# A transformer layer on one core: weights of Q, K and V ahead of later tokens, three gate products on GpSimd, small filling matmuls

## The chip, the cores and the metric

The kernel runs on one core of a Trainium2 chip. The metric is the time of one execution in device microseconds; the runs of the kernel before have a median of 182.08 us.

## The reference

One layer: adaptive layer norm, dilated local attention, a second adaptive norm, a feed-forward block; S = 2048 tokens, D = 448, 16 heads of 28, F = 1792, all in bf16.

```python
mod = (_silu(c) @ w_mod).reshape(c.shape[0], 6, 1, -1)
sa, ca, ga, sb, cb, gb = (mod[:, 0].copy(), ..., mod[:, 5].copy())
h = _layernorm(x, axis=-1) * (1 + ca) + sa
x = x + ga * _A_ref(h, A_wqkv, A_wo)
h = _layernorm(x, axis=-1) * (1 + cb) + sb
x = x + gb * _B_ref(h, B_w1, B_w2)
```

`_A_ref` projects to q, k, v, lets each token attend to itself and the seven even-distance tokens before it (distance 2, 4, ... 14), and projects by `wo`; `_B_ref` is `silu(x @ w1) @ w2`.

## The kernel before, in words

The tokens are cut into four chunks of 512 (k = 0 to 3 in the code; first to fourth below), each held as even and odd tokens, so that the dilated window becomes a dense band in each parity. Attention works on nine blocks of 112 to 128 tokens of a parity. Per chunk there are these stages:

- `Norm` (L443): the statistics of each 128-token tile are taken on VectorE (L455, L456; "b") or on ScalarE (sum L459 and square L465, with the mean on GpSimd at L462 between them; "a"). GpSimd makes the reciprocal root and the scaled shift (L469 to L476), and VectorE or ScalarE writes the normalised tokens `xn` (L485, L483). In the second pair of tiles of the third and fourth chunk the statistics are ScalarE's.
- transposes: the first chunk on TensorE (L513) with scale and shift at L520 and L522; later ones by DMA issued from SP (L535), with scale and shift at L540 and L542. The result is `h`. Scale and shift (`modc`) come from L419, which needs the silu of c; that is turned on TensorE at L404.
- projection: V at L643, Q and K at L619 into pairs of PSUM tiles `ps_qk`; the evacuations are L632 (V) and L623 (Q and K). The Q/K weights are first padded to 32 per head by VectorE (L550, L552).
- attention: logits L671, exponential on ScalarE L679, band mask on VectorE L703, values L729, normalisation L734 and L735, DMA transposes L739, output projection L763 and residual L766.
- feed-forward: L790, silu and evacuation on ScalarE L794, L812, residual L817, store L820.

The gates ga and gb are not applied to the tokens: `wo` and `w2` are multiplied by them once. For `w2` this is L844, seven products of 128 x 896, all on VectorE before.

All PSUM tiles of two banks (`ps_w`, `ps_t`, `ps_v`, `ps_qk`, `ps_l`, `ps_h`, `ps_wo`) come from one pool of three buffers, in turn. A tile that comes third in line waits until the tile before it in that buffer was read.

The order of all work is written out by hand: `ORDER` (L42) lists the operations by number, and `emit` (L195) records them in that order; a "v" or "a" behind a number picks VectorE or ScalarE. Each engine then works through its own queue in that order, and an instruction that waits holds up everything behind it on its engine. Loads are issued by SP at L334. While TensorE has nothing to do at the start, it multiplies a tile of zeros, `junk` (`warm_up`, L387): `WARM` products in one go and ten operations of two each, placed by `ORDER`.

Of the kernel before, what the change touches and what calls it, by code (L numbers as in the profile page):

```python
# [32 lines left out]
CP = 256  # L33
BLOCKS = ((0, 1), (2, 3), (4, 5), (6, 7, 8))
HW = 128 + CP
WARM, JUNK = 7, 10
HOW1 = ("bbbb", "bbbb", "bbaa", "bbaa")
HOW2 = ("ssss", "ssss", "ssss", "ssss")
SEQ = "e0 e1 e2 e3 e4 s0 e5 e6 s1 e7 e8 s2 s3"


ORDER = (  # L42
# [32 lines left out]
def half(j):  # L75
    return slice(K3 * j, K3 * j + K3)
# [140 lines left out]
def layer(ctx, tc, io, safe):  # L217
# [3 lines left out]
    A_x, A_wqkv, A_wo, B_w1, B_w2, c, w_mod, out = io  # L221
    nc = tc.nc
    V, S, G, T = nc.vector, nc.scalar, nc.gpsimd, nc.tensor
# [10 lines left out]
    def ct(shape, name, dt=BF16):  # L234
        return const.tile(shape, dt, name=name)

    def bigt(name):
        return big.tile([128, 2, 512], F32, name=name, tag="big")
# [21 lines left out]
    junk = both[:, KT * 6 * D:KT * 6 * D + 512]  # L260
    w1 = ct([128, 3, F], "w1")
    w13 = ct([128, F // 2], "w13")
    w2 = ct([128, NF, D], "w2")
# [43 lines left out]
    P = Plan()  # L307
# [20 lines left out]
    def sp(ns, fn, deps, land=0.0, give=()):  # L328

        a = P.op(("sp", ns), fn, deps, take=("dma",))  # L330
        return P.op(("none", land), none, [a], give=((a, "dma"),) + tuple(give)), a
# [52 lines left out]

    warm = []

    def warm_up(n):  # L387
        if not warm:
            warm.append(bigt("ps_w"))
        for _ in range(n):  # L390
            T.matmul(warm[0][:, 0, :], lhsT=junk[:, 0:128], rhs=junk, start=True, stop=True)
    w_first = P.op(("pe", 600.0), none, take=("big",))
    w_last = P.op(("pe", 213.0 * WARM), lambda o: warm_up(WARM), [w_first], mac=213.0 * WARM)
    junks = [P.op(("pe", 428.0), lambda o: warm_up(2), [w_last], mac=426.0) for _ in range(JUNK)]

    P.op(("none", 0.0), none, junks, give=((w_first, "big"),))

# [11 lines left out]
    def mod_cols(vecs, dst0, loads):  # L409

        ps = {}

        def mm(o):
            ps[0] = one.tile([128, 2, KT], F32, name="ps_m", tag="one")
            for i, v in enumerate(vecs):
                for j in range(KT):
                    c0 = v * D + ROW[j]
                    for k in range(KT):
                        T.matmul(ps[0][:, i, j:j + 1], lhsT=wmod[:, k, c0:c0 + 128], rhs=scT[:, k:k + 1], start=(k == 0), stop=(k == KT - 1))  # L419

        def ev(o):
            V.tensor_copy(out=modc[:, dst0, :], in_=ps[0][:, 0, :])
            V.tensor_scalar(out=modc[:, dst0 + 1, :], in0=ps[0][:, 1, :], scalar1=1.0, scalar2=None, op0=ALU.add)
        a = P.op(("pe", 900.0), mm, [sct] + loads, take=("one",))
        return P.op(("dve", 150.0), ev, [a], give=((a, "one"),))
# [3 lines left out]
    def gate(i, v, loads):  # L429
        ps = {}  # L430

        def mm(o):
            ps[0] = onet("ps_g")
            for k in range(KT):
                T.matmul(ps[0][:, 0:D], lhsT=screp[:, k, :], rhs=wmod[:, k, v * D:(v + 1) * D], start=(k == 0), stop=(k == KT - 1))
        a = P.op(("pe", 760.0), mm, [rep] + loads, take=("one",), mac=653.0)
        wmod_read.append(a)
        return P.op(either(430.0, 540.0), lambda o: copy_on(o)(out=gbc[:, i, :], in_=ps[0][:, 0:D]), [a], give=((a, "one"),))  # L438
# [154 lines left out]
    def norm1(k):  # L593
        h = h1[k % NH]
        after = [x for kk in (k - NH,) if kk >= 0 for x in qk_mm[kk] + v_mm[kk] + [halo[kk + 1]]] + (pads if k == 2 else [])

        n = Norm([4 * k + j for j in range(4)], {4 * k + j: ld_x[k][j // 2] for j in range(4)}, after=after, n=2, how=HOW1[k], scratch=both[:, KT * 6 * D + 512:KT * 6 * D + 512 + D])

        def out_of(k):
            return h[:, :, k, 128:128 + CP]  # L600
        if k:
            n.on_dma(lambda j: h[:, :, :, 128 + 64 * j:256 + 64 * j].rearrange("p t k s -> p (t k) s"), out_of, 0, [mod1])
        else:
            n.on_pe((0, 2, 1, 3), out_of, lambda ps: ps.rearrange("p (t s) -> p t s", t=2), [mod1], True)
        h1_done[k] = list(n.done)
        if k:
            w = 32 * k
            halo[k] = P.op(either(60.0 + 0.83 * 8 * w, 60.0 + 0.26 * 8 * w), lambda o: copy_on(o)(out=h[:, :, :, 128 - w:128].rearrange("p t k s -> p (t k) s"),
                                                                                               in_=h1[(k - 1) % NH][:, :, :, 128 + CP - w:128 + CP].rearrange("p t k s -> p (t k) s")), h1_done[k - 1] + after)
# [223 lines left out]
    for k in range(NC):  # L833
        norm1(k)
        project(k)
        if k == 0:
            g_o = gate(0, 2, ld_mo)
            g_2 = gate(1, 5, ld_m2)
            mod2 = mod_cols((3, 4), 2, ld_mb)
            wmod_read.append(mod2)  # L840
            wo_gated = [P.op(("dve", 1030.0), lambda o: V.tensor_tensor(out=wo[:, 0], in0=wo[:, 0], in1=gbc[:, 0, :].unsqueeze(1).to_broadcast([128, KT, D]), op=ALU.mult), [g_o] + ld_o)]
            wo_gated += [sp(550.0, f, wo_gated[0:1], 1500.0)[0] for f in (lambda o: nc.sync.dma_start(out=wo[half(1), 1, :, :], in_=wo[half(0), 0, :, :]),
                                                                      lambda o: nc.sync.dma_start(out=wo[half(0), 1, 1:4, :], in_=wo[half(1), 0, 0:3, :]))]
            w2_gated = [P.op(("dve", 535.0), lambda o, f=f: V.tensor_tensor(out=w2[:, f:f + 2, :], in0=w2[:, f:f + 2, :],  # L844
                                                                             in1=gbc[:, 1, :].unsqueeze(1).to_broadcast([128, 2, D]), op=ALU.mult), [g_2, ld_2[f // 8]])
                        for f in range(0, NF, 2)]

# [47 lines left out]
@with_exitstack  # L895
def kernel(
    ctx: ExitStack,
    tc: tile.TileContext,
    A_x: bass.AP,
    A_wqkv: bass.AP,  # L900
    A_wo: bass.AP,
    B_x: bass.AP,
    B_w1: bass.AP,
    B_w2: bass.AP,
    c: bass.AP,
    w_mod: bass.AP,
    out: bass.AP,
):
    io = (A_x, A_wqkv, A_wo, B_w1, B_w2, c, w_mod, out)
    with ExitStack() as first:  # L910
        with tc.manual_schedule():
            bad = layer(first, tc, io, False)
    with tc.If(bad > 0, label="safe"):
        with ExitStack() as again:
            layer(again, tc, io, True)
# [30 lines left out]
```

## Time and profile before

| what | value |
|---|---|
| median of two runs | 182.08 us (181.75 to 182.41) |
| span of the profiled execution, first to last instruction | 179.6 us |
| what lies around the span, by the median | 2.48 us |
| TensorE busy | 168.7 us, 94% of the span |
| VectorE, ScalarE, GpSimd busy | 103.9, 110.1, 26.1 us |
| mean granted TensorE clock | 0.994 |

The profiled execution has no time of its own besides its span. In the profile's rows the engines are PE (TensorE), PEld (its weight loads), DVE (VectorE), ACT (ScalarE), POOL (GpSimd) and SP (SyncE, which issues most DMAs; SPq is its queue). A timeline row has start, length, engine, line, operation, output and inputs, and a count; in square brackets stands how long the engine was idle before it and whose work ended that. TensorE's products are pipelined, so the last of a row shows a tail of some 0.2 to 0.4 us that overlaps the next row. In rows of the chain of waits only start, length, engine, tile and line are given.

### The profile page before, as it was taken

The numbers are of one execution on the slowest core, as the hardware profiler recorded it, in microseconds if no ns is written. First come the engines' busy times: TensorE is split into PE (matmuls) and PEld (weight loads), VectorE is DVE, ScalarE is ACT, GpSimd is POOL, SyncE is SP. The second block draws the span as 40 slices with busy tenths as digits, with TensorE's granted clock in tenths as the row PEclk, the third lists the DMA queues.
The fourth block names the chain that finished last, engine by engine and source line by source line (L and its number), as shares of the span: only waits on it lengthen the run. The fifth ranks groups of instructions, "written<-read, shape, count | busy, mean of one in ns | idle before, by whom it ended". The sixth has DMA issues, their size and how long they took to land.

```text
span 179.6 us, 3554 instructions
## 1 busy us (share of the span) xinstructions
PE 168.7 (94%) x1406; PEld 76.7 (43%) x1406; DVE 103.9 (58%) x219; ACT 110.1 (61%) x153; POOL 26.1 (15%) x86
## 2 busy tenths in 40 slices
PE   7999999888889999999999999999999998999990
PEld 2543333444345344344544445554434444434540
DVE  5699797699798988364378135984633311200211
ACT  2277939897779657779999649643596322244200
POOL 4656540000012220022000000023040000000000
PEclk9999999999999999999999999999999999999997
DMA  5993569956682223102400013125307000010021
GB/s 199 333 344 89 143 143 305 336 117 152 185 251 55 51 62 84 26 0 62 58 26 4 26 26 80 29 55 135 84 0 194 5 0 26 0 51 4 29 79 35
DMA packets 33343, 17.42 MB, mean 97 GB/s; under 512 B 24296, under 2 KB 32936, under 8 KB 33320
## 3 DMA queue, kind: packets, MB, share of 16 engines
q1 hardware_dynamic: 33168, 16.90, 35.0%
q8 instruction: 13, 0.21, 0.5%
q10 hardware_dynamic: 152, 0.23, 0.4%
q14 instruction: 10, 0.08, 0.2%
HBM read 9.12 MB, written 1.84 MB: 61 GB/s over the span
## 4 chain that ended last, share of the span: by engine, by line
PE 70%; DVE 10%; DMA 7%; ACT 6%; POOL 3%; issue 2%; SPq 0%; ACTq 0%; DVEq 0%
PE ps_h L790 25%; PE ps_y L812 24%; PE ps_wo L763 7%; PE ps_qk L619 5%; PE ps_v L643 4%; ACT p L679 2%; PE ps_o L729 2%; DMA oT<-o 2%; DMA x_all<-in_A_x_dram 2%; DVE p L703 2%; DVE st L455 2%; PE ps_l L671 2%; ACT xn L483 2%; DMA wqk<-xn 2%; DMA h<-xn 2%
## 5 line engine op out<-in xcount | busy, mean ns | idle before, releaser
L790 PE MATMUL ps_h<-h,w 128*128 128x512 bf16 (+1 forms) x224 | 47.3, 380 | 0.0
L812 PE MATMUL ps_y<-w,both 128*128 128x448 bf16 x224 | 46.1, 353 | 0.6 <-DVE flag L884 0.6
L794 ACT ACTIVATE both<-ps_h 128x1024 bf16<-128x1024 f32 x28 | 28.0, 1022 | 26.0 <-PE ps_h L790 25.9
L679 ACT ACTIVATE p<-ps_l 128x896 bf16<-128x896 f32 (+1 forms) x36 | 30.7, 933 | 2.2 <-PE ps_l L671 2.1
L812 PEld LDWEIGHTS <-both 128*128 128x128 bf16 x224 | 20.8, 98 | 20.6 <-issue 1.6
L790 PEld LDWEIGHTS <-w 128*128 128x128 bf16 (+1 forms) x224 | 16.9, 96 | 27.0 <-issue 11.4
L817 DVE TENSOR_TENSOR ot<-ps_y,x_all 128x448 bf16<-128x448 f32 x16 | 9.8, 621 | 30.2 <-PE ps_y L812 30.1
L619 PE MATMUL ps_qk<-h,wp 128*128 128x512 bf16 (+1 forms) x96 | 20.0, 380 | 0.4 <-DVE h L542 0.4
L703 DVE TENSOR_TENSOR p<-p,maskb 128x1792 bf16<-128x1792 bf16 (+1 forms) x18 | 19.5, 1098 | 0.5 <-ACT p L679 0.5
L465 ACT ACTIVATE screp<-x_all,mv 128x448 bf16<-128x448 bf16 x16 | 10.7, 666 | 9.9 <-POOL mv L462 9.5
L619 PEld LDWEIGHTS <-wp 128*128 128x128 bf16 (+1 forms) x128 | 9.3, 97 | 16.1 <-issue 6.1
L462 POOL TENSOR_SCALAR mv<-sums 128x2 f32<-128x2 f32 x10 | 3.4, 343 | 76.0 <-DVE x_all L766 75.9
L766 DVE SCALAR_TENSOR_TENSOR x_all<-ps_wo,x_all 128x448 bf16<-128x448 f32 x16 | 9.5, 620 | 7.7 <-PE ps_wo L763 7.7
L485 DVE TENSOR_SCALAR xn<-x_all,mv,rs 128x512 bf16<-128x512 bf16 x23 | 8.8, 406 | 8.6 <-POOL rs L472 8.4
L763 PE MATMUL ps_wo<-wo,oT 128*128 128x448 bf16 (+1 forms) x64 | 12.5, 354 | 1.0 <-DMA oT<-o 0.6
L643 PE MATMUL ps_v<-wv,h 128*128 128x448 bf16 (+1 forms) x56 | 11.1, 354 | 1.0 <-ACT p L679 0.7
L623 DVE CAST qk<-ps_qk 128x1024 bf16<-128x1024 f32 x10 | 12.0, 1214 | 0.1
L472 POOL TENSOR_TENSOR rs<-rs,negh 128x2 f32<-128x2 f32 x16 | 11.5, 717 | 1.3
L735 DVE TENSOR_TENSOR o<-ps_o,rc 112x448 bf16<-112x448 f32 (+1 forms) x18 | 11.2, 624 | 0.6
L729 PE MATMUL ps_o<-v,p 128*128 128x29 bf16 x288 | 9.6, 176 | 1.2 <-DVE gbc L438 0.6
L542 DVE TENSOR_SCALAR h<-h,modc 128x512 bf16<-128x512 bf16 x15 | 5.6, 407 | 8.6 <-DMA h<-xn 8.6
L729 PEld LDWEIGHTS <-p 128*128 128x128 bf16 x288 | 8.8, 96 | 4.1 <-DVE p L703 0.9
(85 smaller groups left out, 147.9 us busy)
## 6 DMA issues: line engine op xcount, KB each, us to landing
out_dram<-ot SPq DMA_DIRECT2D x16, 112.0 KB, 1.7
both<-in_w_mod_dram SPq DMA_DIRECT2D x2, 672.0 KB, 5.7
x_all<-in_A_x_dram SPq DMA_DIRECT2D x3, 448.0 KB, 5.8
w<-in_B_w_dram SPq DMA_DIRECT2D x3, 448.0 KB, 6.0
w<-in_B_w_dram SPq DMA_DIRECT2D x1, 896.0 KB, 5.0
both<-in_w_mod_dram SPq DMA_DIRECT2D x2, 336.0 KB, 3.4
w<-in_B_w_dram SPq DMA_DIRECT2D x1, 672.0 KB, 5.2
wv<-in_A_wqkv_dram SPq DMA_DIRECT2D x2, 224.0 KB, 5.0
```

What stands on the lines that cost most here:

```text
L472: G.tensor_tensor(out=rs[:, j:j + n], in0=rs[:, j:j + n], in1=negh[:, 0:n], op=ALU.pow)
L619: T.matmul(ps[:, j, :], lhsT=w.rearrange("p h d -> p (h d)"), rhs=h[rows, :, t, 128:128 + CP], start=start, stop=stop)
L623: return [(either(act_ns(1024), dve_ns(1024)), lambda o, ps: copy_on(o)(out=qk[:, :, g, :, s0:s0 + CP], in_=ps[:].rearrange("p j (t s) -> ...
L643: T.matmul(ps[:, par, 0:D], lhsT=h[rows, par, t, b0:b0 + 128], rhs=wv[rows, t, :], start=(kk == ks[0]), stop=(kk == ks[-1]))
L679: S.activation(out=out_, in_=ps[:, :, 0:4 * nq].rearrange("p j (g q) -> p j g q", q=nq), func=ACTF.Exp, scale=SCALE)
L703: V.tensor_tensor(out=p, in0=p, in1=maskb[:, 1 if b == 0 else 0, 0:nq].unsqueeze(1).to_broadcast([128, H, nq]), op=ALU.mult)
L729: T.matmul(ps[:, h, 0:DH + 1], lhsT=p[:, at:at + 128], rhs=v[:, h, 0:DH + 1], start=True, stop=True)
L735: V.tensor_tensor(out=box["o"][0:nq, off:off + D].rearrange("p (h d) -> p h d", d=DH), in0=ps[0:nq, :, 0:DH], in1=r.unsqueeze(2).to_broadc ...
L763: T.matmul(ps[:, par, 0:D], lhsT=oT[rows, kk, par, s0:s0 + 128], rhs=wo[rows, par, kk, :], start=(q == qs[0]), stop=(q == qs[-1]))
L790: T.matmul(ps[:, j, :], lhsT=w, rhs=h[rows, :, t, :], start=start, stop=stop)
L794: return [(("act", act_ns(1024)), lambda o, ps: S.activation(out=hid[:, k % 2, :, i, :], in_=ps[:], func=ACTF.Silu), after + f2_read.get(k ...
L812: T.matmul(box["ps"][:, 0:D], lhsT=hid[:, k % 2, f % 2, f // 2, 128 * j:128 * j + 128], rhs=w2[:, f // 2 + 7 * (f % 2), :], start=(f == 0) ...
```

## The change

Three things change.

First, `ORDER`: the loads of the Q, K and V weights (operations 13 to 20 as numbered there) go out right behind the first chunk's tokens and the modulation weights, ahead of the second and third chunk's tokens. The steps that hang on them move too: on VectorE the scale and shift of the first chunk and the padding of the weights now come before the statistics of the second chunk, and on ScalarE the statistics of the third chunk come after the normalisation of the second.

On SP at the start, before:

```order
L334 DMA both<-in_w_mod_dram 64x896
L334 DMA x_all<-in_A_x_dram 128x2x896
L334 DMA wqk_75<-in_A_wqkv_dram 64x448
L334 DMA wv<-in_A_wqkv_dram 128x2x448
L334 DMA x_all<-in_A_x_dram 128x2x896
L334 DMA wv<-in_A_wqkv_dram 128x2x448
L334 DMA wqk<-in_A_wqkv_dram 128x2x896
L334 DMA wqk<-in_A_wqkv_dram 128x2x448
L334 DMA wqk_75<-in_A_wqkv_dram 64x448
```

On SP in the same place, now:

```order
L334 DMA both<-in_w_mod_dram 64x896
L334 DMA wv<-in_A_wqkv_dram 128x2x448 x2
L334 DMA wqk<-in_A_wqkv_dram 128x2x896
L334 DMA wqk<-in_A_wqkv_dram 128x2x448
L334 DMA wqk_75<-in_A_wqkv_dram 64x448 x2
L334 DMA x_all<-in_A_x_dram 128x2x896 x2
```

The tokens of the second and third chunk (`x_all` of 128x2x896) moved behind all six loads of `wv` and `wqk`.

On ScalarE between the first chunk's h and the first table load, before (`both,sums` is L459's sum, `both,mv` L465's square, `v` and `qk` are evacuations):

```order
L520 ACTIVATE h_0_84<-ps_t,modc 128x2x256 x2
L459 ACTIVATE both,sums<-x_all 128x448 x2
L483 ACTIVATE xn_83<-x_all,nm,rs 128x512
L632 CAST v_90<-ps_v 128x32x28
L465 ACTIVATE both,mv<-x_all,mv 128x448
L483 ACTIVATE xn_83<-x_all,nm,rs 128x512 x2
L465 ACTIVATE both,mv<-x_all,mv 128x448
L623 CAST qk<-ps_qk 128x2x2x256 x3
```

On ScalarE in the same place, now (twelve lines were added above, so L520 reads L532 and so on):

```order
L532 ACTIVATE h_0_84<-ps_t,modc 128x2x256 x2
L644 CAST v_90<-ps_v 128x32x28
L495 ACTIVATE xn_83<-x_all,nm,rs 128x512 x3
L471 ACTIVATE both,sums<-x_all 128x448 x2
L477 ACTIVATE both,mv<-x_all,mv 128x448 x2
L635 CAST qk<-ps_qk 128x2x2x256 x3
```

The sums and squares of the third chunk moved behind all three normalisations of the second chunk, and still stand ahead of the evacuations of Q and K.

Second, three of the seven `w2` products, for rows f = 2, 4 and 8, run on GpSimd. On GpSimd around them, before:

```order
L471 TENSOR_SCALAR rs_149<-mv_148 128x2
L472 TENSOR_TENSOR rs_149<-rs_149,negh_113 128x2
L474 TENSOR_TENSOR nm_150<-mv_148,rs_149 128x2
L462 TENSOR_SCALAR mv_148<-sums_115 128x2
L471 TENSOR_SCALAR rs_149<-mv_148 128x2
```

and now:

```order
L483 TENSOR_SCALAR rs_149<-mv_148 128x2
L484 TENSOR_TENSOR rs_149<-rs_149,negh_113 128x2
L486 TENSOR_TENSOR nm_150<-mv_148,rs_149 128x2
L856 TENSOR_TENSOR w2_81<-w2_81,gbc_111 128x896 x3
L474 TENSOR_SCALAR mv_148<-sums_115 128x2
L483 TENSOR_SCALAR rs_149<-mv_148 128x2
```

The three products stand in one piece between two pairs of tiles of the feed-forward norm of the second chunk, ahead of the second pair's mean.

Third, the filling at the start: `WARM` goes from 7 to 5, and four of the ten filling operations become runs of 64, 64, 32 and 32 small products (192 in all; `small_tiles`), on 64x64, 32x64 and 64x128 pieces of the array. On TensorE this makes 5 fills, 192 pieces and 2 fills ahead of L404 (now L416), where 17 fills stood; ten fills between the transposes and the first V projection stay. The filling now takes two PSUM tiles of the pool, both released before the first projection.

```diff
-WARM, JUNK = 7, 10
+WARM, JUNK = 5, 10
...
-    "1 7 2 3 4 75 76 80 84 85 79 61 62 63 74 71 0 5 6 8 9 10 11 12 25 26 99 98 100 68 64 104 103 65 105 101v 106v 72 67 88 77 89 90 108 107v 92 93 102a "
+    "1 7 2 3 4 75 76 80 84 85 79 61 62 63 74 71 0 5 6 8 9 10 11 12 21 22 23 24 13 14 15 16 17 18 19 20 25 26 27 28 99 98 100 68 64 104 103 65 105 101v 106v 72 67 88 77 89 90 108 107v 92 93 102a "
...
+    def small_tiles(rows, cols, n, reps):
+
+        done = 0
+        while done < reps:
+            for r in range(0, 128, rows):
+                for c in range(0, 128, cols):
+                    ps = warm[1 - r // 32 // 2 if rows == 32 else 1][:, r // 32 % 2 if rows == 32 else r // 64, 0:n]
+                    m = min(57, cols) if cols < 128 else 114
+                    T.matmul(ps[c:c + m, :], lhsT=junk[r:r + min(rows, 64) - (4 if rows == 32 else 0), c:c + m], rhs=junk[r:r + min(rows, 64) - (4 if rows == 32 else 0), 0:n], start=True, stop=True)
+                    done += 1
...
-            warm.append(bigt("ps_w"))
+            warm.extend([bigt("ps_w2"), bigt("ps_w")][::-1])
...
-    junks = [P.op(("pe", 428.0), lambda o: warm_up(2), [w_last], mac=426.0) for _ in range(JUNK)]
+    TILES = {3: (64, 64, 29, 64), 7: (32, 64, 57, 64), 8: (64, 128, 29, 32), 2: (64, 64, 57, 32)}
+    junks = [P.op(("pe", 428.0), (lambda o, i=i: small_tiles(*TILES[i])) if i in TILES else lambda o: warm_up(2), [w_last], mac=426.0) for i in range(JUNK)]
...
-            w2_gated = [P.op(("dve", 535.0), lambda o, f=f: V.tensor_tensor(out=w2[:, f:f + 2, :], in0=w2[:, f:f + 2, :],
+            w2_gated = [P.op(("dve", 535.0), lambda o, f=f: (G if f in (2, 4, 8) else V).tensor_tensor(out=w2[:, f:f + 2, :], in0=w2[:, f:f + 2, :],
```

4 rows, old and new, of the table ORDER are left out of this document.

## The prediction

> **What bounds the kernel now.** I read the page's head first, then busy time by stage, then the chain of waits, then the engines' timelines where chain and change meet. The head:
>
> ```profile
> span 179.6 us, 3554 instructions
> ```
>
> The sum is made against this span, 179.6 us; the median of the runs, 182.08, is 2.48 above it, and I add that at the end. By stage (columns: window, its length, busy time of PE, weight loads, DVE, ACT, POOL, granted clock, DMA share, GB/s):
>
> ```profile
> 3.00:5.00 2.00, 2.00 (x6) 0.68 (x5) 1.38 (x9) 0.36 (x1) 0.00 (x0) 1.00 1.03 379
> 30.00:46.00 16.00, 13.81 (x221) 7.34 (x219) 13.29 (x23) 14.03 (x17) 0.00 (x0) 1.00 0.76 209
> 46.00:62.00 16.00, 14.35 (x186) 7.36 (x186) 14.22 (x29) 13.03 (x19) 1.74 (x5) 1.00 0.52 140
> 62.00:84.00 22.00, 22.00 (x142) 9.00 (x138) 14.19 (x28) 15.29 (x24) 4.50 (x12) 1.00 0.22 50
> ```
>
> From 62 us TensorE has no gap to give, so a delay there is not won back. From 30 to 62 it idles 2.19 + 1.65 = 3.84 us, and the chain of waits (start, length, what) runs over other engines:
>
> ```profile
> 13.60 0.20 POOL rs L469
> ...
> 14.98 0.50 POOL nm L476
> ...
> 34.19 1.09 DVE v L632
> ...
> 42.65 3.88 DMA oT<-o
> ```
>
> From 34.19 VectorE's work and then the transposes, landed at 46.53, follow each other without slack, and TensorE and ScalarE do so after them. VectorE's cast at 34.19 waits for the value projection at 32.54 (its row below); what delays that delays the end.
>
> **The start: small pieces.** TensorE's timeline:
>
> ```profile
> 1.25 6.50 PE L391 MATMUL ps_w<-both 128*128 128x512 bf16 x17 [1.25 <-DVE both L289]
> 7.68 0.17 PE L404 MATMUL ps_c<-ident,sc 4*128 4x4 bf16 x1
> 8.10 0.94 PE L419 MATMUL ps_m<-scT,both 128*128 128x1 bf16 x32
> 8.90 1.09 PE L513 MATMUL ps_t<-ident,xn 128*128 128x128 bf16 x12
> 9.83 2.32 PE L391 MATMUL ps_w<-both 128*128 128x512 bf16 x10
> 12.37 3.11 PE L643 MATMUL ps_v<-wv,h 128*128 128x448 bf16 x16 [0.21 <-DVE h L522]
> ```
> ```profile
> 2.08 0.15 PEld L391 LDWEIGHTS <-both 128*128 128x128 bf16 x1 [0.28 <-issue]
> 2.50 0.15 PEld L391 LDWEIGHTS <-both 128*128 128x128 bf16 x1 [0.28 <-issue]
> ```
>
> The first fills start 0.42 us apart, the ten at 9.83 only (2.32 - 0.38) / 9 = 0.216 (0.38 is the tail of the last): TensorE begins at half rate, whatever the granted clock says. Now come 5 fills, 192 pieces and 2 fills ahead of L404. Five at 0.427 end at 3.4. No row has a 64x64 piece; the nearest pairs of load and product are L419's (8.10 to 8.90, 32 in 0.80: 25 ns) and the logits' (84.22 to 84.53 below, 16 in 0.31: 19 ns, in row groups). I take 25 ns, as the pieces are as short and serial as L419's: 192 x 25 ns = 4.8 us, then two fills of 0.216, so L404 starts at 8.6 instead of 7.68. Ends: 19 ns gives 7.5, no delay; double time, as the slow rate makes of the fills, gives 9.6 us and 13.4.
>
> After L404 come its ScalarE copy, 4 transposes (0.31), L419 (0.80) and 12 transposes (about 0.85 unhindered): done at 10.65 instead of 9.99. That is +0.66. The chunk's h is then ready at about 12.1 (ScalarE's half, 1.45 us), and ten fills still stand ahead of L643 on TensorE: 10.6 + 10 x 0.216 = 12.75, against 12.37. If the array stays slow they take 4.27; the buffer wait below hides all but some 0.5 of that.
>
> **Weights first.** The weights were not waited for: VectorE's pads (L550, L552) carry no wait; statistics and a normalisation stand ahead of them.
>
> ```profile
> 12.68 0.61 DVE L455 BATCH_NORM_STATS2 st<-x_all 128x6 f32<-128x448 bf16 x1
> 13.33 0.18 DVE L456 BATCH_NORM_AGGREGATE mv<-st 128x2 f32<-128x6 f32 x1
> 13.43 0.59 DVE L455 BATCH_NORM_STATS2 st<-x_all 128x6 f32<-128x448 bf16 x1
> ...
> 14.46 0.99 DVE L550 COPY wp<-wqk 128x896 bf16<-128x896 bf16 x3
> 15.36 0.27 DVE L552 COPY wp<-wqk 128x448 bf16<-128x448 bf16 x1
> ```
> ```profile
> 11.38 0.57 ACT L459 ACTIVATE both<-x_all 128x448 bf16<-128x448 bf16 x1
> 16.50 1.50 ACT L483 ACTIVATE xn<-x_all,nm,rs 128x512 bf16<-128x512 bf16 x2
> 17.91 0.65 ACT L465 ACTIVATE both<-x_all,mv 128x448 bf16<-128x448 bf16 x1
> 18.57 2.82 ACT L623 CAST qk<-ps_qk 128x1024 bf16<-128x1024 f32 x3
> ```
> ```profile
> 22.30 6.64 PE L619 MATMUL ps_qk<-h,wp 128*128 128x512 bf16 x32 [0.35 <-DVE h L542]
> 32.54 1.61 PE L643 MATMUL ps_v<-wv,h 64*128 64x448 bf16 x8 [0.70 <-ACT p L679]
> ```
>
> On SP two x loads pass behind the weight loads, which are 1.23 MB by their sizes (two of 224, 448, 224 and two of 56 KB): 1.23 MB / 379 GB/s = 3.3 us later (379 stands in the window from 3 to 5 us). The statistics that read them start 3.1 us later themselves (12.7 below, against 13.51 - 4 x 0.75 - 0.9 for h = 9.6), and x was there unwaited before; if that cover is short, it costs one for one. On VectorE, h (0.96) ends at 11.6, pads (14.46 to 15.6, 1.1) at 12.7, four statistics (12.68 to 13.43, 0.75 each) at 15.7; the fourth of this chunk ended at 13.51 before. GpSimd's small steps (13.60 to 15.48, 1.8) put the normalisation at 17.5, and L483's last pair runs 17.5 to 18.95 instead of from 16.50.
>
> ScalarE's queue carries the price. L459's two sums ran at 11.38, in a hole, and L465's squares between other work. Now two sums (0.57 each and their read-outs, 1.35), GpSimd's mean (0.25) and two squares (0.65 each and read-outs, 1.5) all stand behind L483 and ahead of L623: 18.95 + 3.1 = 22.05, against 18.57. TensorE does 24 Q/K products of 0.207 (6.64 / 32) after the value projection's 2.94 (12.75 + 2.94 + 4.97 = 20.66) and then needs the buffer that L623 empties by 23.05. Eight more (1.66) end at 24.7: the second chunk's Q/K starts +2.4 late. Of that the 0.70 wait at 32.54 swallows its part: **+1.7 us** at 34.19 and, by the chain, everywhere after it. Ends: 1.0 with 19 ns pieces (h not late), 6.5 with pieces at double time (4.8 more).
>
> **Gate products on GpSimd.** Rows around 80 us, and GpSimd's prices:
>
> ```profile
> 79.44 0.28 POOL L462 TENSOR_SCALAR mv<-sums 128x2 f32<-128x2 f32 x1
> 79.57 1.15 DVE L844 TENSOR_TENSOR w<-w,gbc 128x896 bf16<-128x896 bf16 x2
> 81.25 0.66 ACT L465 ACTIVATE screp<-x_all,mv 128x448 bf16<-128x448 bf16 x1
> 82.70 1.92 ACT L794 ACTIVATE both<-ps_h 128x1024 bf16<-128x1024 f32 x2
> 84.22 0.38 PE L671 MATMUL ps_l<-qk 28*128 28x112 bf16 x16
> 84.53 3.20 PE L812 MATMUL ps_y<-w,both 128*128 128x448 bf16 x16
> ```
> ```profile
> 1.07 0.29 POOL L292 TENSOR_SCALAR_AFFINE_SELECT ident<-ident 128x128 bf16<-128x128 bf16 x1
> 1.76 0.41 POOL L373 TENSOR_SCALAR_AFFINE_SELECT maskb<-maskb 128x256 bf16<-128x256 bf16 x1
> ```
>
> Taking three products off VectorE earns nothing: between 62 and 84 it is busy 14.19 of 22.00 us and TensorE never waits for it. On GpSimd they stand ahead of L462, whose mean L465 needs, and behind L465 on ScalarE stand the last two evacuations (L794), the table load and all the exponentials. L465 started when ScalarE came free; the mean had been there for 81.25 - 79.72 = 1.53 us. The price of a product is not in the trace. One-operand selects give (0.41 - 0.29) / 128 = 0.94 ns an element and 0.17 fixed: 1.0 us for 896 elements; two operands through the same reader, 1.86. The low end is VectorE's own 0.6 (1.15 for two); the high one 2.5, if each product also waits out a VectorE product of 0.6. I take 1.86, since a product has two operands: 3 x 1.86 = 5.6, so L465 is 5.6 - 1.53 = 4.05 late. ScalarE is nearly solid from there to the exponentials that free the logits' buffers, where TensorE has some 0.1 us in hand: **+3.95 us**. Ends: 0.25 (0.62 each), 5.8 (2.5 each). [...]
>
> **Sum.** 179.6 + 1.7 + 3.95 = 185.25 us of span; with the 2.48 outside it 187.7.
>
> **Rivals.**
> Quick GpSimd: a product runs near VectorE's 0.62 or the one-operand 1.0. For it: the small reads per element; against it: two operands. At 1.0 the late term is 3.0 - 1.53 - 0.1 = 1.4 and the time 182.08 + 1.7 + 1.4 = 185.2, not slower by over 2%. It decides from 1.19 us a product downward: there 1.7 and the late term stay under 3.64 together. Chance 0.20.
> Slow pieces: at half rate a pair takes 50 ns and L404 starts at 13.4: 182.08 + 6.5 + 3.95 = 192.5. For it: the first 5 us visibly run at half rate; against it: 25 ns may be an issue limit that the rate does not touch. Chance 0.17. [...]
> Early work pays: h of the first chunk leaves VectorE sooner, and TensorE's 3.84 idle us before 62 shrink. Against it: ten fills stay ahead of L643, so the start gains 0.2 at most (ten fills from 9.83 end near 12.15), and faster by 2% needs 3.64 of the 3.84. At that point 178.4. Chance 0.04.
> Hidden anyway: GpSimd's mean arrives in time and the start is as now, because pieces and order cost what they replace: 182 to 183. Chance 0.04.
>
> **How the numbers follow.** The forecast has 0.55. Its own range is 186.4 to 189.5. The whole range goes from 184.0 (start +1.7, products at 0.62: +0.25) to 192.5 (slow pieces). About 2% is what a measurement here can tell from no change: 178.4 to 185.7. Faster 0.04; the same is quick GpSimd and hidden, 0.24; slower is the forecast and slow pieces, 0.72.
>
> **What would show it.** Right: L416 (was L404) near 8.6; ScalarE's first Q/K evacuation past 21; a TensorE wait of 2 us for it; three L856 products on GpSimd of 1.9 us; L477 (was L465) waiting for GpSimd's mean near 85, and TensorE idle before the logits. Wrong: L416 by 7.7 or past 10; products under 1.2 us; the second chunk's Q/K at 22.3 as before; or ScalarE running its sums before L495 (was L483).

## The result and the profile after

The changed kernel takes 190.66 us (median of 2 runs, 190.46 to 190.85) against 182.08: a ratio of 1.048, with a 95% interval of 1.042 to 1.053. It is slower by 8.6 us. The profiled execution has 188.9 us of span against 179.6, so 9.3 us are to be found in it; it has 3918 instructions where there were 3554.

TensorE's timeline, the start (start, length, engine, line, operation, tiles, count, and in brackets the idle time ahead and what ended it):

```profile
3.49 3.96 PE L395 MATMUL ps_w<-both 64*57 64x29 bf16 x192
8.35 0.18 PE L416 MATMUL ps_c<-ident,sc 4*128 4x4 bf16 x1
8.86 0.69 PE L431 MATMUL ps_m<-scT,both 128*128 128x1 bf16 x19
10.59 0.49 PE L431 MATMUL ps_m<-scT,both 128*128 128x1 bf16 x13 [1.03 <-issue]
12.60 4.05 PE L402 MATMUL ps_w<-both 128*128 128x512 bf16 x9 [0.22 <-issue]
16.44 3.09 PE L655 MATMUL ps_v<-wv,h 128*128 128x448 bf16 x16
25.27 8.26 PE L631 MATMUL ps_qk<-h,wp 64*128 64x512 bf16 x40 [0.89 <-ACT qk L635]
```

The pieces run at 20.6 ns each on average (3.96 / 192). Then come two things that are not in the sum: TensorE stops for 1.03 us in the middle of L431's 32 products, with no engine to wait for, and the fills behind it (nine of the ten are in the record) start 0.43 us apart, where the ten of before were 0.216 apart. So the value projection starts at 16.44 instead of 12.37. On ScalarE its evacuation (L644) stands ahead of the second chunk's normalisations (L495), and these ahead of the first Q/K evacuation (L635), so the delay goes down ScalarE's queue. These rows of ScalarE, and the chain of waits where the delay reaches VectorE's value cast:

```profile
18.14 0.91 ACT L644 CAST v<-ps_v 128x896 bf16<-128x896 f32 x1 [4.27 <-PE ps_v L655]
18.94 2.23 ACT L495 ACTIVATE xn<-x_all,nm,rs 128x512 bf16<-128x512 bf16 x3
...
24.22 2.82 ACT L635 CAST qk<-ps_qk 128x1024 bf16<-128x1024 f32 x3
```
```profile
36.95 1.62 PE ps_v L655 x8
...
38.60 1.09 DVE v L644
```

The Q/K evacuation is at 24.22 (18.57 before), the cast at 38.60 (34.19): +4.4 us. TensorE's timeline again, at the end of the first half:

```profile
80.42 1.60 PE L775 MATMUL ps_wo<-wo,oT 64*128 64x448 bf16 x8 [1.01 <-DMA oT<-o]
88.33 0.92 PE L824 MATMUL ps_y<-w,both 128*128 128x448 bf16 x4
91.98 0.55 PE L683 MATMUL ps_l<-qk 28*128 28x112 bf16 x14 [2.58 <-ACT both L806]
92.47 4.46 PE L824 MATMUL ps_y<-w,both 128*128 128x448 bf16 x16
```

In the kernel before, this output projection starts right behind its products of L790:

```profile
75.47 1.59 PE L763 MATMUL ps_wo<-wo,oT 64*128 64x448 bf16 x8
```

Now it starts at 80.42, after a wait of 1.01 for a transpose. And before the logits TensorE idles 2.58 us for ScalarE. GpSimd and ScalarE show why, in one timeline each:

```profile
83.22 5.99 POOL L856 TENSOR_TENSOR w<-w,gbc 128x896 bf16<-128x896 bf16 x3
89.18 0.26 POOL L474 TENSOR_SCALAR mv<-sums 128x2 f32<-128x2 f32 x1
```
```profile
89.47 0.67 ACT L477 ACTIVATE screp<-x_all,mv 128x448 bf16<-128x448 bf16 x1 [3.15 <-POOL mv L474]
```

The three products take 5.99 us together, the mean stands behind them, and the square (L477) waits 3.15 us for the mean. After the idle time, 16 products of L824 take 4.46 us instead of 3.20. The granted clock by stretches (window, its length, PE's busy time, clock, DMA share, GB/s):

```profile
91.98:94.40 2.42, 2.42 (x20) 0.50 0.14 33
94.40:96.86 2.46, 2.46 (x12) 0.87 0.33 74
```

The clock stands at 0.50 right behind the wait, and the 16 products take 1.26 us more (4.46 - 3.20).

### The profile page after: what moved, and what is told of

It reads as the page before. It is cut to its first block, busy times and chain, and to the rows that moved or that the text cites. A ratio compares the mean times of both kernels' runs of the same rounds, so it can differ in the third digit from the quotient of the medians.

```text
span 188.9 us, 3918 instructions
## 1 busy us (share of the span) xinstructions
PE 173.4 (92%) x1586; PEld 81.4 (43%) x1588; DVE 107.7 (57%) x216; ACT 110.2 (58%) x153; POOL 31.7 (17%) x89
## 4 chain that ended last, share of the span: by engine, by line
PE 72%; ACT 8%; DVE 7%; POOL 6%; issue 4%; DMA 1%; ACTq 0%
PE ps_y L824 23%; PE ps_h L802 21%; PE ps_v L655 6%; PE ps_wo L775 5%; PE ps_qk L631 5%; PE ps_w L402 4%; POOL w L856 3%; ACT p L691 2%; PE ps_o L741 2%; DVE p L715 2%; PE ps_w L395 2%; PE ps_l L683 2%; ACT xn L495 2%; POOL rs L484 2%; DMA wqk<-xn 1%
## 5 line engine op out<-in xcount | busy, mean ns | idle before, releaser
L824 PE MATMUL ps_y<-w,both 128*128 128x448 bf16 x224 | 47.3, 360 | 0.6 <-DVE flag L896 0.6
L802 PE MATMUL ps_h<-h,w 128*128 128x512 bf16 (+1 forms) x224 | 47.4, 380 | 0.0
L824 PEld LDWEIGHTS <-both 128*128 128x128 bf16 x224 | 21.2, 99 | 21.6 <-issue 3.4
L802 PEld LDWEIGHTS <-w 128*128 128x128 bf16 (+1 forms) x224 | 16.9, 96 | 27.0 <-issue 11.4
L477 ACT ACTIVATE screp<-x_all,mv 128x448 bf16<-128x448 bf16 x16 | 10.7, 668 | 13.0 <-POOL mv L474 12.7
L497 DVE TENSOR_SCALAR xn<-x_all,mv,rs 128x512 bf16<-128x512 bf16 x23 | 12.1, 549 | 10.1 <-POOL rs L484 9.9
L474 POOL TENSOR_SCALAR mv<-sums 128x2 f32<-128x2 f32 x10 | 3.3, 330 | 78.9 <-DVE x_all L778 75.4
L635 DVE CAST qk<-ps_qk 128x1024 bf16<-128x1024 f32 x10 | 12.0, 1214 | 0.0
L683 PE MATMUL ps_l<-qk 28*128 28x112 bf16 (+1 forms) x288 | 7.9, 214 | 3.2 <-ACT both L806 2.6
```

Of the source, the lines that this page charges most:

```text
L497: V.tensor_scalar(out=out_, in0=in_, scalar1=mv[:, j, 0:1], scalar2=rs[:, j:j + 1], op0=ALU.subtract if b else ALU.add, op1=ALU.mult)
L635: return [(either(act_ns(1024), dve_ns(1024)), lambda o, ps: copy_on(o)(out=qk[:, :, g, :, s0:s0 + CP], in_=ps[:].rearrange("p j (t s) -> ...
L802: T.matmul(ps[:, j, :], lhsT=w, rhs=h[rows, :, t, :], start=start, stop=stop)
L824: T.matmul(box["ps"][:, 0:D], lhsT=hid[:, k % 2, f % 2, f // 2, 128 * j:128 * j + 128], rhs=w2[:, f // 2 + 7 * (f % 2), :], start=(f == 0) ...
```

## Experiments

All ratios are against the kernel before, run on the same chip beside each run: its medians there were 181.7 to 182.2 us.

**One part at a time.** The first theory is the prediction's: the early loss comes from ScalarE's queue, hence from the order. Its rival, read off the profile after, is that it comes from the pieces.

The order alone (fills, line 36, and gate products as before; of its three changed lines the first, cut):

```
 ORDER = (
-    ... 0 5 6 8 9 10 11 12 25 26 99 98 100 ...
+    ... 0 5 6 8 9 10 11 12 21 22 23 24 13 14 15 16 17 18 19 20 25 26 27 28 99 98 100 ...
```

> The kernel before with the new order alone: weights first, fills as before, gate products on VectorE. Queue theory (the early loss comes from ScalarE's queue, where the third chunk's sums and squares now stand ahead of the first Q/K evacuation): the value projection starts at 12.4 us at full rate as before, L623 first near 21.5 instead of 18.57, TensorE waits about 2 us for it, and after the 0.70 us wait has swallowed its part the chain is 1.2 us late at the value cast of 34.19: 183.3 us. Array theory (the early loss comes from the pieces: the array is at half rate until 16.4 us, and TensorE stops for 1.03 us): the order is hidden, 182.0 to 182.4 us.

184.02 us, ratio 1.010 (1.006 to 1.014). TensorE's timeline and two steps of the chain of waits, in the slowest of the four executions (184.68 us):

```profile
11.90 3.02 PE L643 MATMUL ps_v<-wv,h 128*128 128x448 bf16 x16
22.60 9.90 PE L619 MATMUL ps_qk<-h,wp 64*128 64x512 bf16 x40 [2.82 <-ACT qk L623]
```
```profile
7.62 4.55 DMA x_all<-in_A_x_dram
...
12.20 0.64 DVE st L455
```

So the order costs 2.1 us with no help from the pieces, and the array theory of the whole early loss falls. The forecast wait for L623 is there, with 2.82 us. Two things came on top. The second chunk's x now lands at 12.17, and its first statistic waits 0.28 us for it. (It starts at 12.20, before at 9.60; the greater part of this is VectorE's own order, in which h and the pads now come first, up to 11.92.) And behind the wait 40 products take 9.90 us, where the same 40 took 8.26 behind the 0.89 us wait of the changed kernel.

The pieces alone (order and gate products as before):

```
-WARM, JUNK = 7, 10
+WARM, JUNK = 5, 10
...
+    TILES = {3: (64, 64, 29, 64), 7: (32, 64, 57, 64), 8: (64, 128, 29, 32), 2: (64, 64, 57, 32)}
```

> The kernel before with the small pieces alone: order and gate products as before. Array theory: the stop near 9.6 us and the fills 0.427 us apart from 12 us are here too, the value projection starts near 16.4 instead of 12.37, and of these 4.1 us some 0.7 to 1.1 are swallowed by waits that are there now: the value cast of 34.19 is 3 to 3.4 us late, 185.1 to 185.5 us. Queue theory: the pieces alone put everything 0.7 us back at most, 182.1 to 182.8 us.

184.69 us, ratio 1.017 (1.013 to 1.022): +2.8 us, a little under the array theory's range and far above the queue theory's. TensorE, in an execution that was the fastest of the four (183.56 us):

```profile
10.32 0.49 PE L431 MATMUL ps_m<-scT,both 128*128 128x1 bf16 x13 [0.76 <-issue]
12.33 2.93 PE L402 MATMUL ps_w<-both 128*128 128x512 bf16 x9 [0.22 <-issue]
15.10 3.02 PE L655 MATMUL ps_v<-wv,h 128*128 128x448 bf16 x16
```

Stop and slow fills belong to the pieces. Here the array sped up within the fills (nine in 2.93), so the value projection came at 15.10; in the profile of the changed kernel, with the same pieces, it came at 16.44.

The GpSimd products alone (order and fills as before):

```
-            w2_gated = [P.op(("dve", 535.0), lambda o, f=f: V.tensor_tensor(
+            w2_gated = [P.op(("dve", 535.0), lambda o, f=f: (G if f in (2, 4, 8) else V).tensor_tensor(
```

> The kernel before with the three gate products on GpSimd alone. The late term as recorded: three products of 1.93 us, 5.8 us ahead of the mean, less 1.53 of slack: L465 at 85.6 instead of 81.25, TensorE idle 2.5 us before the logits, and then, if the array falls to half rate after that idle time as it did in the changed kernel, about 1.0 more: 187.4 us. If the slow array after the idle time belongs to the pieces, 186.4 us. If the loss needs the late start as well, under 185.5.

187.9 us, ratio 1.032 (1.029 to 1.036): +6.0 us, where the highest reading gave 5.3, and needing neither late start nor pieces. TensorE:

```profile
88.73 0.37 PE L671 MATMUL ps_l<-qk 28*128 28x112 bf16 x14 [3.78 <-ACT both L794]
89.03 4.88 PE L812 MATMUL ps_y<-w,both 128*128 128x448 bf16 x16
```

The idle time is 3.78 us, and the slow array behind it costs 1.68 (4.88 - 3.20). The 16 products start 4.50 late (84.53 before); 4.50 + 1.68 = 6.2 us.

**The GpSimd products moved into its idle time.** From the changed kernel, only their place in GpSimd's order is changed:

```
-    ... 481v 145 141 482v 143 142 390 ...
+    ... 368 145 ... 374 143 142 ... 481v 141 482v 390 ...
```

> The changed kernel with its three GpSimd products moved in GpSimd's queue only: one behind the small steps that end at 62.1 us and two behind those that end at 69.6, where GpSimd stands idle for 3.6 and 7.5 us. Queue theory for the late term (the products hurt only because the mean stands behind them): no idle TensorE before the logits, no slow array there, 190.7 - 5.4 = 185.3 us. If the products cost through VectorE, which is held while one runs (2.1 us for a step of 0.41), the wait turns up at VectorE's half of h near 73.3 instead, up to 2 us late: 187 us.

186.45 us, ratio 1.026 (1.022 to 1.029), between the two expectations, since the 5.4 us were too much for the late loss. GpSimd's timeline has the products where they were put; VectorE and TensorE beside the last two:

```profile
61.34 1.96 POOL L856 TENSOR_TENSOR w<-w,gbc 128x896 bf16<-128x896 bf16 x1
...
68.87 3.80 POOL L856 TENSOR_TENSOR w<-w,gbc 128x896 bf16<-128x896 bf16 x2
```
```profile
70.96 2.65 DVE L715 TENSOR_TENSOR p<-p,maskb 128x1792 bf16<-128x1792 bf16 x1
```
```profile
73.67 0.56 PE L741 MATMUL ps_o<-v,p 128*128 128x29 bf16 x16 [0.36 <-DVE p L715]
```

What they still cost there shows beside the changed kernel with all gate products on VectorE (order and pieces together):

> The changed kernel with all gate products back on VectorE: order and pieces together. If GpSimd's products are free once they stand in its idle time, this equals the kernel with the moved products, 186.4 us. If they still cost through VectorE, which is held while one runs (h of the last chunk waited 0.98 us there), 185.0 to 185.6 us. If order and pieces, 2.1 and 2.8 us when each is alone, hide each other, under 185; if they add in full, 186.8.

186.45 us, ratio 1.026 (1.023 to 1.030): the same as with the moved products. So the three products cost 190.66 - 186.45 = 4.2 us in the changed kernel, and moved to where nothing stands behind them on GpSimd they cost nothing that the medians show. In the trace they are not quite free. The mask product at 70.96 takes 2.65 us beside them instead of 1.08, and TensorE waits 0.36 us for it. At 71.72 that profile was 0.78 us ahead of the one without GpSimd products (the value projection had started at 15.20 there, here at 16.44); by the output projection at 80.61 it was 0.11 behind. The expected wait through VectorE is there, then, at some 0.9 us of this execution. The order and the pieces add in the medians: 2.1 + 2.8 = 4.9 against 4.8. TensorE of the kernel without GpSimd products:

```profile
16.44 3.16 PE L655 MATMUL ps_v<-wv,h 128*128 128x448 bf16 x16
80.50 1.60 PE L775 MATMUL ps_wo<-wo,oT 64*128 64x448 bf16 x8 [0.98 <-DMA oT<-o]
89.57 3.20 PE L824 MATMUL ps_y<-w,both 128*128 128x448 bf16 x16
```

L824 starts 5.04 late (84.53 before) and runs at 3.20. In the changed kernel it starts 2.90 later still and takes 1.26 more: 4.16, the 4.2 of the medians, and all of it stands behind the wait for ScalarE, hence behind GpSimd's queue. That the products cost 6.0 alone and 4.2 here fits the 0.98 us wait for the transpose, which delays TensorE but not GpSimd, so that less of GpSimd's delay is left for TensorE to wait out (2.58 against 3.78).

**What in the pieces costs.** The first theory is the stop (TensorE has used up its instructions), the second that small tiles don't bring the array to full rate. 96 pieces of twice the columns in place of 192:

```
-    TILES = {3: (64, 64, 29, 64), 7: (32, 64, 57, 64), 8: (64, 128, 29, 32), 2: (64, 64, 57, 32)}
+    TILES = {3: (64, 64, 58, 32), 7: (32, 64, 114, 32), 8: (64, 128, 58, 16), 2: (64, 64, 114, 16)}
```

> The kernel before with the pieces alone, but 96 of twice the columns in place of 192. Stop theory (the 1 us stop at 9.6 us is TensorE waiting for its next instructions, since 192 loads and 192 products use them up early; and the stop is what keeps the array slow): no stop, no instruction packet ahead of 12 us, the ten fills 0.216 us apart from 10.5, the value projection at 12.4 to 12.8 instead of 15.1, 182.0 to 182.6 us. Tile theory (small tiles don't bring the array to full rate, whatever else happens): no stop either, but the fills still start 0.427 apart, the value projection at 14 to 14.5, 183.3 to 184.3 us.

183.05 us, ratio 1.005 (1.002 to 1.008). No stop, but the fills are slow (ten in 4.23):

```profile
8.17 1.03 PE L431 MATMUL ps_m<-scT,both 128*128 128x1 bf16 x32
10.31 4.23 PE L402 MATMUL ps_w<-both 128*128 128x512 bf16 x10
14.38 3.02 PE L655 MATMUL ps_v<-wv,h 128*128 128x448 bf16 x16
```

The slow rate doesn't need the stop. The packet of the instruction queue that I expected to vanish still came, at 8.2 us, and was not waited for. The next kernels take the whole array for each piece, with 192 and with 96 of them:

```
-                    T.matmul(ps[c:c + m, :], lhsT=junk[r:...
+            T.matmul(warm[1][:, 0, 0:n], lhsT=junk[:, 0:128], rhs=junk[:, 0:n], start=True, stop=True)
```

> The kernel before with 192 pieces that use the whole array, 128 by 128, with the same columns and the same count. Stop theory: the stop at 9.6 us is there as with the small tiles, and the fills behind it start 0.427 apart: the value projection near 15, 184.2 to 185 us. Tile theory: the stop is there, but the array is at full rate by then and stays so, the fills 0.216 apart, the value projection at 12.8 to 13.4, 182.3 to 183.3 us.

185.02 us, ratio 1.014 (1.009 to 1.020). TensorE:

```profile
8.49 0.59 PE L396 MATMUL ps_w<-both 128*128 128x512 bf16 x2
12.18 0.49 PE L425 MATMUL ps_m<-scT,both 128*128 128x1 bf16 x13 [2.13 <-issue]
13.76 3.15 PE L396 MATMUL ps_w<-both 128*128 128x512 bf16 x10
```

Both effects stand apart here. Ahead of the stop two fills take 0.59 = 0.216 + 0.38: full rate. The stop comes after the 19th product of L431's line, as in all the runs with 192 pieces, though later in time; it lasts 2.13 us, and behind it the fills are slow again. So the stop goes by the number of instructions, and this one lost the rate.

> 96 pieces as in the run with half as many, the same count and the same columns, but each on the whole array, 128 by 128; nothing else differs, and no stop is expected in either. Tile theory: the whole-array pieces bring the array to full rate as the fills did, so transposes and fills behind them run at full rate (fills 0.216 us apart) and the value projection starts at 12.2 to 12.6 instead of 14.38: 181.7 to 182.3 us, 0.8 to 1.3 under the narrow pieces. Rival (short pieces of any shape don't count as work for the rate): the fills 0.427 apart, the value projection at 14 to 15, 183 us as with the narrow ones.

182.36 us, ratio 1.004 (1.002 to 1.006). TensorE:

```profile
9.97 2.32 PE L396 MATMUL ps_w<-both 128*128 128x512 bf16 x10
12.41 3.11 PE L649 MATMUL ps_v<-wv,h 128*128 128x448 bf16 x16
```

Same count, same columns as with the 96 narrow pieces, and the fills are at full rate as in the kernel before: the narrow tile keeps the array slow. (The wide pieces also last longer, 4.2 us against 2.5, but 192 narrow ones lasted 4.0 and did not bring the rate about either.) In time it can't be told from the narrow ones (the intervals overlap, against an expected 0.8 or more), so a value projection 2.0 us late by itself costs little; what the remaining 0.4% of both is stays open.

So the price goes with the count. 96 pieces cost 0.9 us narrow and 0.5 wide; 192 cost 2.8 either way. Beside the stop a second loss comes with 192: the transpose ahead of the output projection near 80. The DMA view of that stretch (76.3 to 80.4 us) in the changed kernel, and from 72.5 to 75.4 in the kernel before:

```profile
q8 instruction: 1, 0.02, 1.6%
...
oT<-o SPq DMA_TRANSPOSE x1, 3.8
```
```profile
oT<-o SPq DMA_TRANSPOSE x1, 2.3
```

From issue to landing the transpose takes 3.8 us instead of 2.3, and one packet of the instruction queue moves meanwhile. It is so in all six profiles with 192 pieces, where TensorE then waits 0.94 to 1.48 us; in the eight others no such packet moves there, the transpose takes 2.3, and TensorE does not wait. So some 1 us of the price of the pieces falls 70 us behind them. That the packet is what delays the transpose is inferred from this coincidence.

**The order's price.** The third chunk's sums, mean and squares go behind the first chunk's Q/K evacuations, on the order alone and on order and pieces:

```
-    ... 184 185 190 189 191 193 223 ... 197 198 192 225 194 ... 122a 123 ...
+    ... 184 185 223 ... 197 198 225 ... 122a 123 190 189 191 193 192 194 ...
```

> The kernel before with the new order alone (184.0 us), but with the third chunk's two sums, GpSimd's mean and the two squares put behind the first chunk's three Q/K evacuations on ScalarE. Queue theory (those 3.1 us ahead of L623 are the price of the order): L623 first at 18.6 to 19.2 instead of 22, TensorE's wait of 2.82 us is gone, and of the 2.1 us of the order 1.2 to 2 come back: 182.0 to 182.8 us. Landing theory (the price is the second chunk's x, which now lands at 12.2 behind the weights and starts the statistics, the normalisation and the transposes late): 183.6 to 184.3 us.

184.44 us, ratio 1.012 (1.008 to 1.016), the same as without the move (1.010). TensorE:

```profile
14.80 6.63 PE L619 MATMUL ps_qk<-h,wp 128*128 128x512 bf16 x32
23.06 3.41 PE L619 MATMUL ps_qk<-h,wp 128*128 128x512 bf16 x16 [1.62 <-DVE h L542]
27.69 3.45 PE L619 MATMUL ps_qk<-h,wp 128*128 128x512 bf16 x16 [1.22 <-DVE qk L623]
```

> Order and pieces without the GpSimd products, with the third chunk's sums, mean and squares behind the first chunk's Q/K evacuations. Queue theory: TensorE's wait of about 1.5 us for L635 goes, the second chunk's Q/K starts 1.5 us earlier, and 1 to 1.5 us come back against the kernel without this move. Successor theory (what the move frees is taken by the next wait, the third chunk's normalisation and h, as with the order alone): within 0.5 us of the kernel without this move.

187.71 us, ratio 1.032 (1.029 to 1.036): 1.3 us slower than without the move. The queue theory falls as the price of the order. The wait for L623 goes as expected, and the next ones stand right behind it: the second chunk's h (its statistics now stand behind the first chunk's h and the pads on VectorE) and the evacuations of VectorE, whose third-chunk work now came late. ScalarE's queue was the last wait, and moving this work behind it does not pay. No run took back VectorE's part of the order, or the late x, by itself, so what the order's 2.1 us are due to is narrowed down, not shown.

**A step taken out of the start.** The kernel before with ScalarE's normalisation of the second chunk ahead of a square of the third:

```
-    "191 127a 193 157a 156a 128 19 20 ...
+    "191 127a 157a 156a 193 128 19 20 ...
```

> The kernel before with one step moved: on ScalarE the second chunk's second normalisation (L483 at 16.50) stands ahead of the third chunk's square (L465 at 15.84) instead of behind it. Theory: the start is a chain over the second chunk's statistics, normalisation, transposes and h, so 0.8 us of ScalarE work taken out of it starts h at 20.1 instead of 20.86, TensorE loses its waits of 0.35 and part of the 0.70, and the end comes 0.5 to 0.9 us earlier, 181.2 to 181.6 us. Rival: the normalisation's inputs or the transposes' queue hold it where it is, 182.0 us.

181.48 us, ratio 0.998 (0.996 to 0.9996): at most 0.4% faster, less than expected. TensorE, and its chain of waits:

```profile
15.13 13.10 PE L619 MATMUL ps_qk<-h,wp 128*128 128x512 bf16 x64
46.23 1.60 PE L763 MATMUL ps_wo<-wo,oT 128*128 128x448 bf16 x8 [1.25 <-DMA oT<-o]
```
```profile
33.17 1.09 DVE v L632
...
44.97 5.67 DMA w<-in_B_w_dram
...
50.66 1.16 DVE w L844 x2
```

The start did get shorter: 64 Q/K products without a wait, the value cast at 33.17 instead of 34.19. The 1.02 us is lost again by 53: the first output projection waits 1.25 us for transposes (46.23, where before had 46.57), and VectorE, ready sooner for its two gate products, has to wait for the w2 load (the DMA named w), which lands at 50.64. With h of the first chunk ahead of the statistics as well:

```
-    ... 111 113a 17 18 ... 81 87 112v 154 ...
+    ... 111 113a 112v 17 18 ... 81 87 154 ...
```

> The same, and on VectorE h of the first chunk ahead of the second chunk's three statistics, as the change has it, without moving any load. Rival of the prediction (early work pays): h is there 1.5 us earlier, the value projection starts when the ten fills end, 12.15, and the gain is 0.2 us at most beyond the kernel with one step moved, 181.0 to 181.6. If the statistics, 0.96 us later for it, put the second chunk's normalisation and transposes back, it is 0.3 to 0.9 us slower than that kernel, 181.9 to 182.4.

181.69 us, ratio 1.000 (0.998 to 1.002). "Early work pays" gets nothing: neither its gain nor the delay of the statistics can be told from no change.

## Why the prediction was right, and where its sum was not

The forecast was slower, 187.7 us; the time is 190.66, 3.0 above the point. It lies above the forecast's own range, 186.4 to 189.5, and inside the whole range, whose upper end of 192.5 came from "Slow pieces", a rival whose condition did not occur. The direction and the late mechanism were right; that the time fell inside the range is in part luck.

1. Late term, +3.95: the mechanism held at each link (products on GpSimd, the mean behind them, the square behind the mean, the evacuations, the logits). A product took 2.00 us in the group (5.99 / 3) where 1.86 was taken. What is due to them in the changed kernel is 4.2 us. The term came near this by two errors that cancel: 2.90 of delay instead of 3.95, and 1.26 of half-rate array that it did not have. "Quick GpSimd" is out.
2. Early term, +1.7: measured 4.8 (order and pieces together), and this is the step that was mis-sized. It counted the order at its ScalarE wait and the pieces at +0.66 us ahead of h, and it said of a slow array that "the buffer wait below hides all but some 0.5 of that". It does not hide it: the evacuation of V (L644) stands on ScalarE ahead of the normalisations, so the queue that was to hide the late value projection is itself late. L495 starts at 18.94, where the sum has 17.5 for the last pair, and L635 at 24.22, where it has 22.05. The pieces alone cost 2.8. L416 came at 8.35, before the forecast 8.6, so the price per piece (25 ns; 20.6 measured) was not the fault. What the sum left out or took for hidden is the stop, the rate that the pieces failed to raise, and the 1 us at the transpose. With 96 narrow pieces the rate is as low, but the value projection is only 2.0 us late, and they cost 0.9; here it is 4.1 us late. (4.8 and 4.2 make 9.0 against the measured 8.6, since the kernel before ran at 181.68 beside the one and at 182.08 beside the other.)
3. The order was priced nearly right, 2.1 alone. The ScalarE wait was there, but it is not the price: taking it away returned nothing, since the next waits stood right behind it. In the profiled execution the 40 products behind the wait lost 1.64 us more (9.90 - 8.26) to the half rate, which the sum did not have. The cover for x, of which the prediction says "if that cover is short, it costs one for one", was short by 0.28 us in the order-alone kernel.
4. "+1.7 us at 34.19 and, by the chain, everywhere after it": the delay was 4.4 us at the value cast, had fallen to 3.8 by the output projection at 50.41 (46.57 before), and stayed there up to 74, where the start of L802 was 3.77 late (74.47 against 70.70 in the chains). At 80 the transpose put some 1.2 on top (80.42 against 75.47), which the terms did not have and which came with the 192 pieces.
5. "Slow pieces" was given 192.5 with 0.17. Its condition (a pair at 50 ns) was wrong: the pieces took 20.6 ns each. Its result, a slow array that delays the start by 4 us, came about in another way.

## What to carry to other kernels

Ask of each added instruction what stands behind it on its own queue: the same three GpSimd products cost 4.2 us ahead of a mean and nothing that the medians show 14 to 22 us earlier, where GpSimd was idle. Filling work for TensorE had to be wide here to bring the array to full rate (ten fills took 2.32 us behind 96 wide pieces, 4.23 behind 96 narrow ones), and few in instructions: 192 pieces brought a stop of 0.76 to 2.13 us and a late transpose (3.8 us instead of 2.3), 96 did not. And a wait that ends last is not yet a price: take it away once, and see what stands next.

## What the runs showed of the hardware

The array's rate. The trace keeps a record of the granted clock, which the views average; where it has no entry yet, they print 1.00. Its first entry, at full clock, stands at 6.66 us in the kernel before, where the fills double their rate (0.42 us apart ahead of it, 0.216 from 9.83 on). In the changed kernel it stands at 16.55, just behind the start of the value projection (16.44), and the fills ahead of it are 0.43 apart. In these two profiles every later change of the clock lies a whole number of steps of 3.41 us behind the first entry: 50 steps in the kernel before, 22, 23 and 50 in the changed one, where step 50 is behind TensorE's last product in both.

What brought the array to full rate went by the kind of piece. The two fills right behind the pieces took 0.59 us with whole-array pieces, 192 (5.30 us of them) or 96 (4.2), and 1.03 us with 96 narrow ones (2.5 us of them). Behind the 192 narrow pieces of the changed kernel, 3.96 us of them, the nine fills on record from 12.60 on still took 4.05 us.

Four profiles lost the rate again behind a wait. In the changed kernel the clock fell to 0.50 at 91.65, during the wait of 2.58 us, for one step of 3.41. The others show it in their products: ten fills in 3.15 us instead of 2.32 behind the wait of 2.13, 40 products in 9.90 instead of 8.26 behind that of 2.82, 16 products in 4.88 instead of 3.20 behind that of 3.78. The mean granted clock of these four profiled executions is 0.986 to 0.989, that of the others 0.994 or more. A wait of 1.90 us (order and pieces, Q/K first) did not do it: the 16 products behind it took 3.45 us, 16 others in that profile 3.41. What sets the rate was not shown beyond this.

Instructions. With 192 pieces TensorE stopped after the same instruction in each of the six profiles, for 0.76 to 2.13 us, and never with 96. A packet of the instruction queue began to move some 2.4 us before the stop ended: at 8.1 us in the changed kernel (10.59), at 9.7 with the 192 whole-array pieces (12.18). That the wait is for that packet is argued from these times, not shown.

VectorE beside GpSimd. While the three products ran, VectorE's steps took four to five times as long:

```profile
83.16 2.09 DVE L497 TENSOR_SCALAR xn<-x_all,mv,rs 128x512 bf16<-128x512 bf16 x1
85.17 2.30 DVE L856 TENSOR_TENSOR w<-w,gbc 128x896 bf16<-128x896 bf16 x1
```

L497 takes 0.41 us alone (L485 of before), L856 0.58 (L844 of before, 1.15 for two). What holds VectorE there was not shown. In the changed kernel TensorE did not wait for VectorE in that stretch; with the moved products it did, for 0.36 us.
